# Attention and two gated layers on one core: first loads in another order, early weight conversions placed one head later

## The chip, the cores and the metric

The kernel runs on one core of a Trainium2 chip. The metric is the device time of one execution in microseconds (us); the median of three runs of the kernel before is 1163.88 us.

## The reference, cut to what matters

Four batches of 8 heads, 576 tokens, head width 64: causal attention with a bias from running sums of `s`, then two gated layers of width 512 and inner width 1536 over all 2304 tokens.

```python
scores = scale * np.matmul(q, k.transpose(0, 1, 3, 2))
cum = np.cumsum(np.maximum(s, 0.0), axis=-1)
bias = -(cum[:, :, :, None] - cum[:, :, None, :])
scores = np.where(causal, -1e9, scores + np.minimum(bias, 0.0))
attn = softmax(scores)
x = np.matmul(attn, v)            # -> [2304, 512]
x = (sigmoid(x @ w_gate) * (x @ w_val)) @ w_out
return ((x @ w_a) * (x @ w_b)) @ w_out2
```

The weights arrive as 8-byte floats; the kernel converts them to pairs of 4-byte parts (high and low).

## The kernel before, in words

The kernel has two stages one after the other: `attention()`, 32 heads, and `mlps()`, the two layers. Both write their work as named operations of a `Schedule` (line 27): an engine, a function, the operations that it depends on, and a priority, which is a planned time. For attention the operations are given out with `in_order=True` (lines 47 to 69): of all operations whose dependences have been given out, the one with the smallest priority goes next. So the priority alone sets the order in which each engine (TensorE, VectorE, ScalarE, GpSimd) and each queue of DMA issues works, and every one of them works strictly in that order. An instruction that waits holds back all that stands behind it on its engine. SyncE (SP) issues nearly all loads; ScalarE issues two small transfers per head.

Priorities are counted in planned heads of `HT` = 6.1; head i starts at `t0 = HT * i`. For each head there are, in the order of the data:

- `lqk` (load_qk, line 337) brings q and k of a head into one of three tiles `r`; `lv` (lines 341, 342) brings v in two DMAs into one of two tiles `vx`;
- `hq1`, `hk1` (lines 472, 473) round them on ScalarE into `o`; `hk2`, `hq2` (474, 475) copy them by DMA into the second tile; `lok`, `loq` (476, 478) write the rounding rests on VectorE. The load of q and k for head i waits for these four of head i-3;
- `rel` (482, 483) brings the bias rows of a head by two DMAs. For the first three heads `relk` and `relq` (416, 439) write them directly from the running sums (`sums`, lines 406 to 411, then `relh` 434 and `rell` 435);
- `S` (498, 503): TensorE makes scores in two groups, `mx` (511): VectorE takes their maxima, `mT` (518) turns them, `mc` (520) copies them on ScalarE, `md` (522) sends them by DMA into `o`;
- `ST` (535, 536): scores again, transposed; `ex` (541): exp on ScalarE; `cs` (557): causal mask on GpSimd; `pv` (570): times v; `xc` (579) copies out, `sd`, `rd`, `rb` (581, 603, 600) bring the row sums round by DMA, and `xm` (583) divides on GpSimd.

The score groups share one PSUM tile, so group 1 of a head can start only when the maxima of group 0 are taken, and the next head's group 0 only after those of group 1.

Among the heads, eleven weight tiles are prepared (`weights`, line 253; the loop at 609): one load (line 205 or 210, 512 KB, SP queue) every three heads, with priority `HT * (3 * e - 2)` for tile e, and then steps: `mag` (224, ScalarE), two steps into `u` (225, 227, VectorE), two more on VectorE (229, 232), the copy (243, ScalarE) and the rest (244, GpSimd). Their places are the entries of the list `at`, counted from the load's place: the first three steps stood one head after the load, the next two two and three heads after it.

At the very start, SP issues `s` (line 403, read once per group of rows, so four times over), then q and k of three heads, then the constants of the first two heads (`selectors`, lines 380, 381, two DMAs each), whose data GpSimd makes.

Of the kernel before, what the change touches and what calls it, by code (L numbers as in the profile page):

```python
# [22 lines left out]
def f32(ap):  # L23
    return ap.bitcast(FP32)


class Schedule:
# [9 lines left out]
    def op(self, name, eng, dur, fn, deps, prio, acq=None, rel=None, lat=None):  # L37
        rel = () if rel is None else rel if isinstance(rel[0], tuple) else (rel,)
        self.ops[name] = (eng, dur, fn, deps, prio, acq, rel, self.LAT if lat is None else lat)
# [80 lines left out]
def attn_mlp_kernel(  # L120
# [14 lines left out]
    nc = tc.nc  # L135
# [39 lines left out]
    early = [(i, m) for m in range(2) for i in range(3)] + [(3, 0), (3, 1)]  # L175
# [77 lines left out]
    def weights(sc, n, m, deps, prio, part=None, at=None):  # L253


        key = (n, m)
        steps = w_steps(n, m)
        nv = len(steps) - 2
        prev = ("wl",) + key
        sc.op(prev, "SP", 0.0 if part == 1 else 0.5, lambda: None if part == 1 else w_load(n, m), deps, prio,  # L260
              acq=("raw", key), lat=0.0 if part == 1 else WLAT)
        for k, (eng, d, fn) in enumerate(steps):
            if part is not None and (k < nv) != (part == 0):
                continue
            last = k == len(steps) - 1
            name = ("wr" if last else "w%d" % k,) + key
            sc.op(name, eng, d, fn, [prev], prio + (at[k + 1] if at else 0.01 * k), acq=("u", key) if nv and k == 0 else None,
                  rel=(("u", key),) if nv and k == nv - 1 else ("raw", key) if last else None)
            prev = name
# [20 lines left out]
    def attention():  # L290
        with ExitStack() as c2:
            def tile1(shape, dtype, name):
                return alone(c2, shape, dtype, name, side="right")
# [12 lines left out]
            NO, NR2, NX = 4, 3, 5  # L306
# [19 lines left out]
            o_t = [tile1([128, CK1 + S], F32R, f"o{i}") for i in range(NO)]  # L326
# [7 lines left out]
            sel, neg1 = ya_sb[0:NR, 1, 2 * S:3 * S], ya_sb[0:3, 1, 3 * S:4 * S]  # L334

            def load_qk(i):
                nc.sync.dma_start(out=r_t[i % NR2], in_=qk[i])

            def load_v(i):
                v, e = vx_t[i % 2], i % 2  # L340
                nc.sync.dma_start(out=v[:, 0:4, e * D:(e + 1) * D], in_=vm[i // 4, :, i % 4])
                nc.sync.dma_start(out=v[0:TL, 4, e * D:(e + 1) * D], in_=vt[i // 4, :, i % 4])
# [36 lines left out]
            def selectors(o):  # L379
                nc.sync.dma_start(out=f32(o[D:R1, CQ1:CQ1 + S]), in_=sel[:, None].to_broadcast([NR, 2, S]))  # L380
                nc.sync.dma_start(out=f32(o[R1:KB + 1, CK1:CK1 + S]), in_=neg1)
# [10 lines left out]
            op = sc.op  # L392
# [34 lines left out]
            op("ms1", "Pool", 1.2, lambda: nc.gpsimd.memset(f32(o_t[1][D:2 * D]), 0.0), ["masks"], -270)  # L427
            op("mkb", "ACT", 0.7, masks_b, ["masks"], -280)
            for j in range(NR2):
                op(("lqk", j), "SP", 0.6, lambda j=j: load_qk(j), ["s"], -290 + j, lat=3.0)  # L430
            for j in range(2):
                op(("sel", j), "SP", 1.3, lambda j=j: selectors(o_t[j]), [("lqk", j), "selc", "ms1"], -260 + j, lat=2.2)
            op("sums", "DVE", 2.7, sums, ["s"], -250)
            op("relh", "ACT", 0.67, lambda: nc.scalar.copy(out=rel[:, 0], in_=cum), ["sums"], -230)
            op("rell", "DVE", 0.7, lambda: nc.vector.tensor_tensor(
                out=rel[:, 1], in0=cum, in1=f32(rel[:, 0]), op=ALU.subtract), ["relh"], -220)
            op("more", "DVE", 5.0, more, ["rell"], -219)
            for i, (name, eng) in enumerate((("Pool", nc.gpsimd), ("ACT", nc.scalar), ("SP", nc.sync))):
                op(("relk", i), "SP", 0.65, lambda i=i: nc.sync.dma_start(
                    out=f32(o_t[i][D:R1, CK1:CK1 + S]), in_=f32(rel[i:NR * BH:BH])), ["rell", "more"], -210 + i, lat=2.2)  # L440
                for c in range(NR):
                    op(("relq", i, c), name, 0.6, lambda i=i, c=c, eng=eng: relq(eng, i, c), ["rell", "more"], -200 + i, lat=2.2)
            for c in range(NR):
                op(("rels", c), "Pool", 0.6, lambda c=c: relq_store(c), ["rell"], -20, lat=2.2)
            op("relk", "SP", 1.2, lambda: nc.sync.dma_start(
                out=relk_d.rearrange("b c e s -> c b e s"), in_=f32(rel)), ["rell"], -190, lat=2.5)
# [5 lines left out]
            HT = 6.1  # L452
# [5 lines left out]
            def head(i):  # L458
                b, h = divmod(i, H)
                t0 = HT * i  # L460
                o, o2, r, vx, pt = o_t[i % NO], p_t[i % 3], r_t[i % NR2], vx_t[i % 2], pt_t[i % 3]
                nm, mr = nm_t[i % 4], mr_t[i % 3]
                k1, q1, k2, q2 = o[:, CK1:CK1 + S], o[:, CQ1:CQ1 + S], o2[:, S:2 * S], o2[:, 0:S]
                up, dn = slice(0, D), slice(D, 2 * D)
                done = [("ST", i - NO, c) for c in range(NC)] + [("S", i - NO, g) for g in range(2)]
                done2 = [("ST", i - 3, c) for c in range(NC)]

                if i >= NR2:
                    op(("lqk", i), "SP", 0.7, lambda: load_qk(i),
                       [(w, i - NR2) for w in ("hq1", "hk1", "lok", "loq")], t0 - 4 * HT + 4.6, lat=3.0)  # L470
                op(("lv", i), "SP", 0.9, lambda: load_v(i), [("pv", i - 2, 1), ("sel", 1)], t0 + 4.0, lat=3.0)
                op(("hq1", i), "ACT", 0.65, lambda: nc.scalar.copy(out=q1[up], in_=r[up]), [("lqk", i)] + done, (-255, -229, -228)[i] if i < NR2 else t0 - 3 * HT + 5.2)
                op(("hk1", i), "ACT", 0.65, lambda: nc.scalar.copy(out=k1[up], in_=r[dn]), [("lqk", i)] + done, (-255, -229, -228)[i] if i < NR2 else t0 - 3 * HT + 5.2)
                op(("hk2", i), "ACT", 0.7, lambda: nc.scalar.dma_start(out=f32(k2[dn]), in_=f32(k1[up])), [("hk1", i)] + done2, t0 - 2 * HT + 0.05)
                op(("hq2", i), "SP", 0.5, lambda: nc.sync.dma_start(out=f32(q2[up]), in_=f32(q1[up])), [("hq1", i)] + done2, t0 - 2 * HT + 0.1)
                op(("lok", i), "DVE", 0.9, lambda: nc.vector.tensor_tensor(
                    out=k2[up], in0=r[dn], in1=f32(k2[dn]), op=ALU.subtract), [("hk2", i)], t0 - HT + 3.0)
                op(("loq", i), "DVE", 0.9, lambda: nc.vector.tensor_tensor(
                    out=q2[dn], in0=r[up], in1=f32(q1[up]), op=ALU.subtract), [("hq1", i)] + done2, t0 - HT - 0.5)
# [11 lines left out]
                for g, cs in ((0, (3, 2, 0)), (1, (1, 4))):  # L491
# [31 lines left out]
                    out=f32(o[KB:KB + 1, CQ1:CQ1 + 640]), in_=f32(mr)), [("mc", i)] + done, t0 - HT + 3.6, lat=2.2)  # L523
# [39 lines left out]
                def pv(reg):  # L563
# [14 lines left out]
                x, j = xt[i % NX], i // 2  # L578
# [5 lines left out]
                    out=x_sb[own, h // 2, b * S:(b + 1) * S], in0=x[own], in1=rb_t[j % 2][own], op=ALU.mult),  # L584
# [21 lines left out]
            for i in range(NH):  # L606
                head(i)

            for e, key in enumerate(order[:len(early) + NRAW]):
                split = [3 * HT + 1.6, 3 * HT + 4.6] if e < len(early) else [0, 0]  # L610
                weights(sc, *key, [("S", 3 * e - 3, 0)], HT * (3 * e - 2), part=None if e < len(early) else 0,
                        at=[0, HT + 1.2, HT + 1.9, HT + 2.5, 2 * HT + 1.9, 3 * HT + 1.9] + split)

            for k in range(KD):
                t0 = HT * (NH - 12 + k)
                op(("x0h", k), "ACT", 0.4, lambda k=k: nc.scalar.copy(out=xs0[:, 0, k], in_=x_sb[:, k, 0:NB]), [("xm", i) for i in range(H)], t0 + 1.7)
                op(("x0l", k), "DVE", 0.5, lambda k=k: nc.vector.tensor_tensor(
                    out=xs0[:, 1, k], in0=x_sb[:, k, 0:NB], in1=f32(xs0[:, 0, k]), op=ALU.subtract), [("x0h", k)], t0 + 2.6)
# [157 lines left out]
    with tc.manual_schedule():  # L776
        attention()
        mlps()
# [45 lines left out]
```

## Time and profile before

| | |
|---|---|
| runs of the kernel before | 1162.53, 1163.88, 1164.17 us |
| profiled execution | 1162.06 us, its span 1160.3 us |
| attention | about 0 to 245 us of the span |
| the two layers | to 1160 us |
| TensorE busy, whole span | 1104.7 us (95%) |
| VectorE, ScalarE, GpSimd busy | 633.2, 357.3, 294.7 us |

Times in the rows are microseconds from the start of the span. A line of the timeline gives start, duration, engine, line of the kernel, operation, what is written and read, and in brackets how long the engine stood idle before and what ended that. SPq and ACTq are the issue queues of SyncE and ScalarE; a DMA's duration there is that of its issue, not of its data.

### The profile page before, as it was taken

The numbers are of one execution on the slowest core, as the hardware profiler recorded it, in microseconds if no ns is written. First come the engines' busy times: TensorE is split into PE (matmuls) and PEld (weight loads), VectorE is DVE, ScalarE is ACT, GpSimd is POOL, SyncE is SP. The second block draws the span as 40 slices with busy tenths as digits, with TensorE's granted clock in tenths as the row PEclk, the third lists the DMA queues.
The fourth block names the chain that finished last, engine by engine and source line by source line (L and its number), as shares of the span: only waits on it lengthen the run. The fifth ranks groups of instructions, "written<-read, shape, count | busy, mean of one in ns | idle before, by whom it ended". The sixth has DMA issues, their size and how long they took to land.

```text
span 1160.3 us, 16120 instructions
## 1 busy us (share of the span) xinstructions
PE 1104.7 (95%) x6152; PEld 1038.0 (89%) x6152; DVE 633.2 (55%) x1015; ACT 357.3 (31%) x635; POOL 294.7 (25%) x364
## 2 busy tenths in 40 slices
PE   1699989999999999999999999999999999999998
PEld 1587777788999999999999999899999999999997
DVE  4787887728323694337963358622487334653322
ACT  2475665634222441113321124322243111221100
POOL 2245445454100341002420023310133111211100
PEclk9999999999999999999999999999999999999999
DMA  3566665614100231001320012200033000200001
GB/s 102 130 165 170 166 162 148 167 52 127 38 1 1 74 109 37 1 1 55 100 64 1 1 38 91 91 1 1 20 95 105 1 1 1 73 28 28 28 28 55
DMA packets 69743, 74.08 MB, mean 64 GB/s; under 512 B 28551, under 2 KB 53311, under 8 KB 69666
## 3 DMA queue, kind: packets, MB, share of 16 engines
q1 hardware_dynamic: 66514, 68.08, 20.1%
q10 hardware_dynamic: 2896, 4.81, 1.8%
q8 instruction: 49, 0.80, 0.3%
q14 instruction: 28, 0.23, 0.1%
q0 software_dynamic: 256, 0.15, 0.1%
HBM read 57.65 MB, written 5.60 MB: 55 GB/s over the span
## 4 chain that ended last, share of the span: by engine, by line
PE 76%; DVE 8%; DMA 6%; issue 4%; POOL 3%; ACT 1%; SPq 1%; ACTq 0%; POOLq 0%; DVEq 0%
PE ps L277 23%; PE ps L278 23%; PE ps L276 23%; PE ps_x L570 4%; PE ps_g L498 1%; DVE u L227 1%; DVE u L225 1%; DMA raw<-in_moe_w_out_dram 1%; POOL w L244 1%; DVE h L716 1%; DVE raw L232 1%; DVE hf L702 1%; DVE raw L229 1%; POOL x_sb L583 1%; PE ps_e L535 1%
## 5 line engine op out<-in xcount | busy, mean ns | idle before, releaser
L276 PE MATMUL ps<-xs,w 128*128 128x384 f32 x1152 | 385.0, 334 | 0.0
L278 PE MATMUL ps<-xs,w 128*128 128x384 f32 x1152 | 385.0, 334 | 0.0
L277 PE MATMUL ps<-xs,w 128*128 128x384 f32 x1152 | 384.9, 334 | 0.0
L713 POOL TENSOR_SCALAR h<-hf 128x384 fp32r<-128x384 f32 x144 | 92.1, 640 | 576.5 <-DVE hf L702 576.5
L702 DVE TENSOR_TENSOR hf<-ps,g 128x384 f32<-128x384 f32 x144 | 80.0, 555 | 280.9 <-PE ps L278 278.5
L276 PEld LDWEIGHTS ps<-xs,w 128*128 128x128 f32 x1152 | 216.3, 188 | 0.7
L277 PEld LDWEIGHTS ps<-xs,w 128*128 128x128 f32 x1152 | 216.2, 188 | 0.7
L278 PEld LDWEIGHTS ps<-xs,w 128*128 128x128 f32 x1152 | 216.2, 188 | 0.0
L698 ACT ACTIVATE g<-ps 128x384 f32<-128x384 f32 x144 | 70.7, 491 | 434.2 <-PE ps L278 434.1
L716 DVE TENSOR_TENSOR h<-hf,h 128x384 fp32r<-128x384 f32 x144 | 88.9, 618 | 83.0 <-POOL h L713 83.0
L244 POOL TENSOR_TENSOR w<-raw,w 128x512 fp32r<-128x512 f32 x72 | 99.8, 1387 | 133.1 <-ACT w L243 128.6
L276 PE MATMUL ps<-h,w 128*128 128x384 f32 x288 | 97.3, 338 | 2.4 <-POOL h L713 1.8
L278 PE MATMUL ps<-h,w 128*128 128x384 f32 x288 | 97.0, 337 | 1.8 <-POOL w L244 1.8
L570 PE MATMUL ps_x<-pt,vx 128*128 128x320 f32 (+4 forms) x448 | 97.2, 369 | 1.1 <-ACT xt L579 1.0
L277 PE MATMUL ps<-h,w 128*128 128x384 f32 x288 | 97.1, 337 | 0.6 <-DVE h L716 0.6
L570 PEld LDWEIGHTS ps_x<-pt,vx 128*128 128x128 f32 x448 | 77.2, 194 | 18.8 <-ACT xt L579 1.3
L511 DVE TENSOR_REDUCE nm<-ps_g 128x1 f32<-128x512 f32 (+4 forms) x160 | 77.0, 531 | 29.4 <-PE ps_g L503 29.4
L277 PE MATMUL ps<-w,h 128*128 128x512 f32 x216 | 84.6, 392 | 1.0 <-POOL w L244 0.9
L276 PE MATMUL ps<-w,h 128*128 128x512 f32 x216 | 84.1, 389 | 0.3 <-ACT w L243 0.3
L278 PE MATMUL ps<-w,h 128*128 128x512 f32 x216 | 84.4, 391 | 0.0
L498 PE MATMUL ps_g<-o 128*128 128x512 f32 (+2 forms) x192 | 45.2, 346 | 40.3 <-DVE nm L511 18.4
L557 POOL TENSOR_SCALAR_AFFINE_SELECT pt<-pt 128x256 f32<-128x256 f32 (+1 forms) x96 | 48.7, 526 | 129.1 <-ACT pt L541 127.8
(92 smaller groups left out, 1323.1 us busy)
## 6 DMA issues: line engine op xcount, KB each, us to landing
raw<-in_moe_w_out_dram SPq DMA_DIRECT2D x24, 512.0 KB
r<-in_qk_dram SPq DMA_DIRECT2D x32, 288.0 KB
raw<-in_moe_w_gate_dram SPq DMA_DIRECT2D x12, 512.0 KB
raw<-in_moe_w_val_dram SPq DMA_DIRECT2D x12, 512.0 KB
raw<-in_moe_w_a_dram SPq DMA_DIRECT2D x12, 512.0 KB
raw<-in_moe_w_b_dram SPq DMA_DIRECT2D x12, 512.0 KB
o<-o ACTq DMA_DIRECT2D x32, 144.0 KB
o<-o SPq DMA_DIRECT2D x32, 144.0 KB
```

The costliest lines, as they stand in the source:

```text
L244: ("Pool", 1.23, lambda: nc.gpsimd.tensor_tensor(out=wtile(n, m)[:, 1], in0=value(), in1=f32(wtile(n, m)[:, 0]), op=ALU.subtract)),
L276: nc.tensor.matmul(out=outp, lhsT=wh, rhs=xh, start=(e == 0), stop=False)
L277: nc.tensor.matmul(out=outp, lhsT=wh, rhs=xl, start=False, stop=False)
L278: nc.tensor.matmul(out=outp, lhsT=wl, rhs=xh, start=False, stop=(e == n - 1))
L498: nc.tensor.matmul(out=ps[0:n, p0 + k0:p0 + k0 + kn], lhsT=q1[:, 128 * c:nk], rhs=k1[:, k0:k0 + kn], start=c in first or (c == 4 and k0 == ...
L511: nc.vector.tensor_reduce(out=nm[0:n, c:c + 1], in_=ps[0:n, p0:p0 + nk], axis=AX.X, op=ALU.max)
L557: nc.gpsimd.affine_select(to, to, [[0, 2], [1, n]][2 - w:], ALU.is_ge, 0.0, base=0, channel_multiplier=-1)
L570: nc.tensor.matmul(out=px[:, 256 + a:256 + q1_], lhsT=vx[:, j], rhs=pt[:, p0:p0 + q1_ - a], start=j == 0, stop=j == js[-1])
L698: op(("g", i, c), "ACT", 0.06 + N * 0.00083, lambda c=c, g=g: nc.scalar.activation(out=sc.get("g", (i, c))[:, 0:N], in_=sc.get("ps", g)[:, ...
L702: op(("hf", i, c), "DVE", 0.07 + N * 0.00104, lambda c=c, u=u: nc.vector.tensor_tensor(out=sc.get("hf", (i, c))[:, 0:N], in0=sc.get("ps", ...
L713: op(("hh", i, c), "Pool", 0.245 + N * 0.00083, lambda c=c, src=src: nc.gpsimd.tensor_scalar(sc.get("h", (i, c))[:, 0, 0:N], src(), 1.0, 1 ...
L716: op(("hl", i, c), "DVE", 0.07 + N * 0.00104, lambda c=c, src=src: nc.vector.tensor_tensor(out=sc.get("h", (i, c))[:, 1, 0:N], in0=src(), ...
```

## The change

Three things move; nothing is added or removed. At the start, the constants of the first head are issued ahead of q and k of head 0, those of the second head ahead of q and k of heads 1 and 2, and the constants no longer name the load of q and k among their dependences. The load of v is placed at 4.8 instead of 4.0 within its head, which is behind the head's issue of `sd` (4.5) and of `lqk` (4.6) instead of ahead of them. And all seven conversion steps of the weights stand one `HT` later, while their loads stay where they are.

```diff
             for j in range(NR2):
-                op(("lqk", j), "SP", 0.6, lambda j=j: load_qk(j), ["s"], -290 + j, lat=3.0)
+                op(("lqk", j), "SP", 0.6, lambda j=j: load_qk(j), ["s"], -259.5 + j, lat=3.0)
             for j in range(2):
-                op(("sel", j), "SP", 1.3, lambda j=j: selectors(o_t[j]), [("lqk", j), "selc", "ms1"], -260 + j, lat=2.2)
+                op(("sel", j), "SP", 1.3, lambda j=j: selectors(o_t[j]), ["selc", "ms1"] if j else ["selc"], -260 + j, lat=2.2)
...
-                op(("lv", i), "SP", 0.9, lambda: load_v(i), [("pv", i - 2, 1), ("sel", 1)], t0 + 4.0, lat=3.0)
-                op(("hq1", i), "ACT", 0.65, ..., (-255, -229, -228)[i] if i < NR2 else t0 - 3 * HT + 5.2)
-                op(("hk1", i), "ACT", 0.65, ..., (-255, -229, -228)[i] if i < NR2 else t0 - 3 * HT + 5.2)
+                op(("lv", i), "SP", 0.9, lambda: load_v(i), [("pv", i - 2, 1), ("sel", 1)], t0 + 4.8, lat=3.0)
+                op(("hq1", i), "ACT", 0.65, ..., (-251, -229, -228)[i] if i < NR2 else t0 - 3 * HT + 5.2)
+                op(("hk1", i), "ACT", 0.65, ..., (-251, -229, -228)[i] if i < NR2 else t0 - 3 * HT + 5.2)
...
-                split = [3 * HT + 1.6, 3 * HT + 4.6] if e < len(early) else [0, 0]
+                split = [4 * HT + 1.6, 4 * HT + 4.6] if e < len(early) else [0, 0]
                 weights(sc, *key, [("S", 3 * e - 3, 0)], HT * (3 * e - 2), part=None if e < len(early) else 0,
-                        at=[0, HT + 1.2, HT + 1.9, HT + 2.5, 2 * HT + 1.9, 3 * HT + 1.9] + split)
+                        at=[0, 2 * HT + 1.2, 2 * HT + 1.9, 2 * HT + 2.5, 3 * HT + 1.9, 4 * HT + 1.9] + split)
```

## Rows read from the trace of the kernel before

**Rows 1.** Busy time by stretch: start:end, length, engines' busy us, granted clock, DMA share, GB/s

```profile
60.00:100.00 40.00, 40.00 (x247) 33.41 (x246) 32.93 (x61) 27.70 (x52) 18.98 (x27) 1.00 0.65 168
100.00:235.00 135.00, 123.60 (x735) 101.58 (x733) 108.66 (x191) 81.27 (x152) 65.88 (x86) 0.99 0.62 161
...
171.00:176.00 5.00, 5.00 (x20) 3.59 (x19) 3.83 (x8) 2.08 (x5) 3.89 (x4) 0.66 0.65 159
275.00:1160.00 885.00, 877.58 (x4838) 848.91 (x4837) 441.82 (x670) 210.82 (x367) 172.58 (x200) 1.00 0.12 40
```

**Rows 2.** Timeline, the first 20 us

```profile
0.80 0.76 SPq L403 DMA_DIRECT2D ya_sb<-in_s_dram  x1
...
1.61 1.37 SPq L337 DMA_DIRECT2D r<-in_qk_dram  x3
...
3.61 0.75 SPq L380 DMA_DIRECT2D o<-ya_sb  x1
...
8.48 0.46 DVE L406 TENSOR_SCALAR ya_sb<-ya_sb 128x576 f32<-128x576 f32 x1 [4.97 <-DMA ya_sb<-in_s_dram]
...
9.08 0.67 ACT L472 CAST o<-r 64x576 fp32r<-64x576 f32 x1 [4.71 <-DMA r<-in_qk_dram]
...
11.42 0.67 ACT L434 CAST ya_sb<-ya_sb 128x576 fp32r<-128x576 f32 x1 [0.99 <-DVE ya_sb L411]
...
16.95 1.19 PE L498 MATMUL ps_g<-o 128*128 128x512 f32 x3 [16.95 <-DMA o<-ya_sb]
```

**Rows 3.** DMA, first 12 us in 40 slices of 0.3 us: GB/s

```profile
GB/s 0 0 0 0 0 0 0 31 8 77 200 261 353 207 207 146 246 346 215 200 207 207 161 92 54 69 84 100 100 100 100 100 100 100 31 0 0 0 0 0
```

**Rows 4.** Timeline, 22 to 43 us: the first weight tile and heads 0 to 2

```profile
22.67 0.37 PE L518 MATMUL ps_t<-idf,nm 128*5 128x128 f32 x1 [1.26 <-DVE nm L511]
...
25.33 0.95 SPq L205 DMA_DIRECT2D raw<-in_moe_w_gate_dram  x1
26.32 2.78 SPq L475 DMA_DIRECT2D o<-o  x2
32.07 0.68 ACT L224 ACTIVATE mag<-raw 128x512 f32<-128x512 f32 x1 [17.32 <-DMA raw<-in_moe_w_gate_dram]
32.08 0.43 DVE L225 TENSOR_SCALAR u<-raw 128x512 int32<-128x512 int32 x1 [9.55 <-DMA raw<-in_moe_w_gate_dram]
32.54 0.69 DVE L227 SCALAR_TENSOR_TENSOR u<-raw,u 128x512 int32<-128x512 int32 x1
...
33.26 0.75 DVE L476 TENSOR_TENSOR o<-r,o 64x576 fp32r<-64x576 f32 x1
...
33.94 1.34 DVE L511 TENSOR_REDUCE nm<-ps_g 128x1 f32<-128x512 f32 x3
...
35.33 1.06 PE L498 MATMUL ps_g<-o 128*128 128x256 f32 x3 [10.78 <-DVE nm L511]
...
39.49 0.78 PE L535 MATMUL ps_e<-o 128*128 128x512 f32 x1
...
42.44 0.63 PE L498 MATMUL ps_g<-o 128*128 128x256 f32 x3
```

**Rows 5.** TensorE's waits, 60 to 250 us: us in total, times, longest

```profile
PE ps_g L498 <- DVE nm L511: 6.2, 5, 2.3
PE ps_g L498 <- DMA o<-relq_d: 3.4, 3, 2.0
```

**Rows 6.** VectorE's waits, 60 to 250 us: for weight tiles

```profile
DVE u L225 <- DMA raw<-in_moe_w_gate_dram: 3.2, 2, 1.7
DVE u L225 <- DMA raw<-in_moe_w_out_dram: 3.0, 2, 2.0
```

**Rows 7.** The SP queue's waits, 60 to 235 us

```profile
SPq L342 <- DMA o<-mr: 14.3, 6, 4.1
SPq L581 <- DMA raw<-in_moe_w_gate_dram: 5.7, 3, 2.9
```

**Rows 8.** Timeline, 95 to 108 us: the issue of a load of v

```profile
104.16 0.48 SPq L342 DMA_DIRECT2D vx<-in_vt_dram  x1
```

More of the change, by code (lines that the diff above doesn't have):

```diff
@@ L470, in head @@
                        [(w, i - NR2) for w in ("hq1", "hk1", "lok", "loq")], t0 - 4 * HT + 4.6, lat=3.0)
-                op(("lv", i), "SP", 0.9, lambda: load_v(i), [("pv", i - 2, 1), ("sel", 1)], t0 + 4.0, lat=3.0)
-                op(("hq1", i), "ACT", 0.65, lambda: nc.scalar.copy(out=q1[up], in_=r[up]), [("lqk", i)] + done, (-255, -229, -228)[i] if i < NR2 else t0 - 3 * HT + 5.2)
-                op(("hk1", i), "ACT", 0.65, lambda: nc.scalar.copy(out=k1[up], in_=r[dn]), [("lqk", i)] + done, (-255, -229, -228)[i] if i < NR2 else t0 - 3 * HT + 5.2)
+                op(("lv", i), "SP", 0.9, lambda: load_v(i), [("pv", i - 2, 1), ("sel", 1)], t0 + 4.8, lat=3.0)
+                op(("hq1", i), "ACT", 0.65, lambda: nc.scalar.copy(out=q1[up], in_=r[up]), [("lqk", i)] + done, (-251, -229, -228)[i] if i < NR2 else t0 - 3 * HT + 5.2)
+                op(("hk1", i), "ACT", 0.65, lambda: nc.scalar.copy(out=k1[up], in_=r[dn]), [("lqk", i)] + done, (-251, -229, -228)[i] if i < NR2 else t0 - 3 * HT + 5.2)
                 op(("hk2", i), "ACT", 0.7, lambda: nc.scalar.dma_start(out=f32(k2[dn]), in_=f32(k1[up])), [("hk1", i)] + done2, t0 - 2 * HT + 0.05)
```

## The prediction

> **What bounds the kernel now.** I read the busy times by stretch first. From 275 us on, the two layers keep TensorE busy 877.58 of 885.00 us, and nothing of the change lies there, so whatever attention saves or loses reaches the end whole [rows 1]. Within attention TensorE is busy 40.00 of 40.00 us from 60 to 100, and 123.60 of 135.00 from 100 to 235 [rows 1]. So there are two places to gain: the first 40 us, in which TensorE has hardly begun, and some 11 us of holes after 100.
>
> Next the timeline of the start. TensorE's first scores begin at 16.95, when the bias rows have landed; these come from the sums over s, which wait for s until 8.48, and ScalarE starts on q and k of head 0 at 9.08 [rows 2]. The DMA rate shows why s is late: between 200 and 353 GB/s in the burst of s and three loads of q and k, then a flat 100 GB/s from 8.1 to 10.2 [rows 3]. Then TensorE stands idle for 10.78 us before 35.33. Its releaser is a maximum on VectorE, but that is only the end of a queue: VectorE stood 9.55 us and ScalarE 17.32 us in front of the first weight tile, which SP issued at 25.33 and which landed at 32.07 [rows 4]. Behind it stood the copy `mc` of head 0, `lok` of head 0 (33.26) and the maxima of head 1 (33.94), none of which needs a weight [rows 4].
>
> Last the waits after 60 us. TensorE waits 6.2 us in five places for maxima and 3.4 us in three for bias rows [rows 5]; VectorE waits 3.2 and 3.0 us in four places for weight tiles [rows 6]; SP waits long for landings of transfers that its next DMA doesn't read, 14.3 us for `md` before the second half of v, 5.7 us for a weight tile before `sd` [rows 7]. I read that as a limited number of landings that can be outstanding: a slow weight load holds up whatever is issued some places behind it.
>
> **The change part by part: first loads.** Now s goes alone. It is 128 rows of 2304 bytes, 295 KB. At the flat 100 GB/s it takes 2.9 us; first bytes move at 2.1 to 2.4 us [rows 3], so it lands near 5.6 instead of 8.46. At the burst's 353 GB/s it would be 3.4, and without any gain 8.46; I take 5.6, since the flat rate is that of few transfers left over. The sums took 8.48 to 11.42 [rows 2], so they end at 8.6. But the next step, `relh` on ScalarE, stands behind `hq1` and `hk1` of head 0. Their load is issued behind two DMAs of constants, 3.61 plus twice about 0.8, at 5.2 [rows 2]; with the same 1.4 us to its first bytes and 200 GB/s it lands at 8.1, at 100 GB/s at 9.5. Two steps of 0.67 [rows 2] make `relh` start at 9.5 (bound: 10.9) instead of 11.42. I take 1.7 us earlier, between 0.5 and 1.9, for the first scores, and for everything that SP issues behind the bias rows: the weight load at 23.6, landed by the same 6.74 us [rows 4] at 30.3. The constants' wait for GpSimd costs nothing: SP waited until 3.61 for it before too [rows 2].
>
> **The first weight tile.** Its step `mag` gets priority 1.2, which puts it behind `mc` of head 0 (-2.55) and ahead of `mc` of head 1 (3.55); the first step into `u` gets 1.9, behind the second maxima of head 1 (0.7) and ahead of `lok` of head 1 (3.0). So `mc` of head 0 follows its transpose at 22.67 + 0.37 - 1.7 = 21.3, `lok` of head 0 and the maxima of head 1 follow without the weights, and VectorE reaches `u` near 27. There it still waits, some 3.3 us instead of 9.55. From 30.3: 0.43 + 0.69 for the two steps, 0.75 for `lok` and 1.34 for the maxima of head 2 [rows 4] end at 33.5, and the second scores of head 2 start at 33.6 instead of 42.44 [rows 4]. TensorE comes out the same way: the transposed scores of head 0 need `hq2`, issued right behind the weight load on SP, so about 30.5, and the group took 42.44 - 39.49 = 2.95 us [rows 4]: 33.5. ScalarE's exp waits for q and k of head 3, issued near 27.5 and landing about 2 us behind the weights, plus 1.34 us of rounding: 33.7. Three engines agree within half a microsecond: 42.44 - 33.6 = 8.8; I take **8.6**, 1.7 from the first loads and 6.9 from here. If s brings only 0.5 it is 7.4; if all of 1.9, 8.8. From there TensorE is full [rows 1], so the shift stays.
>
> **The other conversions.** The ten later tiles' steps are as many and as long; each set meets one head later, when the load has landed. That takes away VectorE's 6.2 us of waits [rows 6] and ScalarE's beside them. What it is worth to TensorE lies between 0 and the 6.2 us that it waited for maxima [rows 5]; I take **3.0**, half, because the waits for bias rows come from another queue and will end later than some of the removed ones: 3.4 us of them are there already [rows 5]. The single `u` and `mag` stay free in time (released at 4 HT + 1.9, next taken at 5 HT + 1.2), as do the three `raw` tiles. The last tile's step on VectorE lies at 32 HT, ahead of the last reciprocal at 34 HT: hidden; uncovered it would be 0.7 us.
>
> **The load of v** goes behind `sd` and q and k on SP. Where SP waits for `sd` (ScalarE's copy out), the two issues of v, 0.48 each [rows 8], no longer fill that wait and `hq2` and the bias rows go out up to 1.0 us later. Where SP is held by a weight tile's landing, it's v that is held, which has about a head to spare, and no longer q and k. I take 0 for both together, with ends of +1.0 per weight load at worst and -1 in all at best.
>
> Sum: 8.6 + 3.0 = 11.6 us. The profiled execution took 1162.06 us (span 1160.3), 1.8 below the median; 1162.06 - 11.6 = 1150.5, and against the median of 1163.88 it is **1152.3**.
>
> **The rivals.** (a) *SP paces the middle.* The conversions' waits go, but the bias rows, behind the weight load on SP, end TensorE's waits a moment later. For it: SP's long waits for landings [rows 7], and that TensorE's holes begin only after 100 us though weights are loaded before, as if slack were used up [rows 1]. Against: TensorE's larger waits are for maxima [rows 5]. Gain 8.6 alone: 1155.3.
>
> (b) *s lands no earlier alone.* The load of s may be held by the few DMA engines that serve it, whatever runs beside it. The flat 100 GB/s at the end of the burst [rows 3] would then be its own pace all along. `relh` then starts at 8.48 + 2.94 = 11.42 as before, the 1.7 go, and 6.9 + 3.0 give 1154.0. Against: 295 KB at 100 GB/s end at 5.4, not 8.46, so something beside it slowed it. The Trainium skill, page DMA: Bandwidth & Descriptors, section Rules for kernel authors, says that a leading broadcast dimension of c copies confines a DMA to at most c engines; s has four such copies. By that rule q and k on the other engines would leave s alone, and the sum would be 9.9 instead of 11.6.
>
> (c) *All holes go.* TensorE's waits for maxima and bias rows, 6.2 + 3.4 [rows 5], vanish, and with them the stretch at a granted clock of 0.66 from 171 to 176, (1 - 0.66) x 5 = 1.7 us [rows 1]: 8.6 + 9.6 + 1.7 = 19.9, 1144.0. Against: the bias rows' queue isn't relieved.
>
> (d) *The first wait only moves.* VectorE and ScalarE still stand before the first tile until 30.3. If what stands behind them then (`lok` of head 1, `mc` of head 1, q and k of head 4) is the true start of the pipeline, only the 1.7 and the two steps' 1.1 plus one set of maxima of 1.3 are won: 4.1, 1159.8. Against: the work behind the wait was head 0's and head 1's [rows 4], which now goes ahead of it.
>
> (e) *Given back.* From 60 us on the DMAs move 168 and 161 GB/s [rows 1]; if that were the limit over all of attention, the start would be won and lost again later: within 2 us of 1163.9. Against: a share of 0.65 busy, 0.62 later.
>
> (f) *Slower.* v behind q and k puts the bias rows 1.0 us later in each head with a weight load. It decides where those rows already end TensorE's wait [rows 5], and where a wait grows long enough to bring the clock to half, as at 171: 8 loads x (1.0 + 1.7) = 21.6, less 8.6: 1176.9. It needs four such heads to eat the start. Against: one such stretch in all of attention before [rows 1].
>
> **How the numbers follow.** A measurement here can tell about 0.2%, 2.3 us. Chances: the forecast 0.39, (a) 0.25, (b) 0.12, (c) 0.10, (d) 0.06, (e) 0.05, (f) 0.03. The first five, 0.92, are faster; (e) is no change; (f) slower. The forecast's own range is 1149 to 1155; a range of 1145 to 1160 takes in (a), (b), (d) and what of (c) stops short of all holes, and leaves out (e) and (f).
>
> **What would show it.** Right: TensorE's idle of 10.78 us gone, the second scores of head 2 near 33.6, VectorE's first wait for a weight tile 2 to 4 us and none after it; the first sums near 5.6; q and k at ScalarE near 8.1. Wrong: sums still at 8.5 (b), TensorE's waits for bias rows grown from 3.4 to 6 us or more (a), more stretches of half clock (f). The forecast fails if the second scores of head 2 come after 36, or if the holes from 100 to 235, then 8 us earlier, stay at 11 us.

## The result and the profile after

The changed kernel takes 1150.15 us (median of 4 runs, 1149.07 to 1154.16) against 1163.2 us for the kernel before (median of 4 runs). The ratio on record is 0.9895, 95% interval 0.9869 to 0.9922; the two medians by themselves give 0.9888. The profiled execution took 1150.44 us, its span 1148.7: 11.6 us less than the profiled execution before, and 11.6 us was the sum of the forecast. The sum came out, but not every term of it; the parts of this section say which.

**The start.** The timeline of the kernel after, its first 42 us (columns as in [rows 2]; an SPq line is the issue of a DMA):

```profile
6.50 0.46 DVE L406 TENSOR_SCALAR ya_sb<-ya_sb 128x576 f32<-128x576 f32 x1 [2.99 <-DMA ya_sb<-in_s_dram]
...
8.19 0.67 ACT L472 CAST o<-r 64x576 fp32r<-64x576 f32 x1 [3.82 <-DMA r<-in_qk_dram]
...
8.87 0.67 ACT L473 CAST o<-r 64x576 fp32r<-64x576 f32 x1
8.89 0.52 DVE L411 TENSOR_SCALAR ya_sb<-ya_sb,small 128x576 f32<-128x576 f32 x1
9.57 0.67 ACT L434 CAST ya_sb<-ya_sb 128x576 fp32r<-128x576 f32 x1
...
15.12 1.19 PE L498 MATMUL ps_g<-o 128*128 128x512 f32 x3 [15.12 <-DMA o<-ya_sb]
...
20.72 0.75 DVE L476 TENSOR_TENSOR o<-r,o 64x576 fp32r<-64x576 f32 x1
...
23.36 0.87 SPq L205 DMA_DIRECT2D raw<-in_moe_w_gate_dram  x1
...
29.09 0.43 DVE L225 TENSOR_SCALAR u<-raw 128x512 int32<-128x512 int32 x1 [2.35 <-DMA raw<-in_moe_w_gate_dram]
...
30.23 0.76 PE L536 MATMUL ps_e<-o 128*128 128x512 f32 x1 [0.64 <-DMA o<-o]
...
33.04 1.04 PE L498 MATMUL ps_g<-o 128*128 128x256 f32 x3
...
35.88 1.19 PE L498 MATMUL ps_g<-o 128*128 128x512 f32 x3
...
37.07 0.78 PE L535 MATMUL ps_e<-o 128*128 128x512 f32 x1
```

The sums over s begin at 6.50 instead of 8.48 [rows 2]. `relh` (L434) begins at 9.57 instead of 11.42 and now stands right behind `hk1`, which ends at 9.54; the sums end just ahead of that, at 9.41. The first scores begin at 15.12 instead of 16.95. The weight load is issued at 23.36 instead of 25.33 [rows 4]. The work that stood behind the first weight tile goes ahead of it: `lok` of head 0 at 20.72 instead of 33.26 [rows 4]. VectorE's wait at `u` shrinks from 9.55 to 2.35 us, and TensorE's hole of 10.78 us is gone: 0.64 us is left, in front of `hq2`'s copy at 30.23.

**A part of that is not kept.** The second scores of head 2 begin at 33.04 instead of 42.44, 9.4 us earlier. The first product with v, some 8 us of work later, is only 6.6 us earlier. TensorE's rows at the end of that work, first after, then before:

```profile
40.32 1.04 PE L498 MATMUL ps_g<-o 128*128 128x256 f32 x3
...
41.55 2.98 PE L570 MATMUL ps_x<-pt,vx 128*128 128x256 f32 x14
```

```profile
44.76 0.70 PE L498 MATMUL ps_g<-o 128*128 128x512 f32 x3
...
45.40 0.48 PE L535 MATMUL ps_e<-o 128*128 128x512 f32 x1
...
48.14 2.98 PE L570 MATMUL ps_x<-pt,vx 128*128 128x256 f32 x14
```

The scores of head 3 took 0.70 us before (at 44.76) and 1.19 after (at 35.88); the first transposed scores behind them 0.48 and 0.78. So this work ran at the lower of TensorE's two levels, 1.2 GHz, where it ran at 2.4 GHz before. The durations fall to the fast ones at about the same time in both kernels: the 128x256 scores take 1.06 us at 35.33 and 0.63 at 42.44 before [rows 4], and 1.04 us still at 40.32 after. The trace's first entry of the granted clock, at full speed in both, stands at 42.08 us before and at 41.44 after. (The busy times read 1.00 from 30 to 42 us all the same, because the time ahead of the first entry is counted as 1.00.) The change brought the work forward, but not the clock.

From the second scores of head 2 to the first product with v it is 8.51 us after (33.04 to 41.55) and 5.70 before (42.44 to 48.14). The busy times of that stretch (columns as in [rows 1]) after, before, and in x3, the kernel before with only v moved:

```profile
33.04:41.55 8.51, 7.25 (x31) 5.68 (x30) 4.83 (x9) 5.66 (x10) 2.51 (x4) 1.00 0.65 182
42.44:48.14 5.70, 4.40 (x31) 3.43 (x30) 4.61 (x8) 3.15 (x7) 3.16 (x4) 1.00 0.76 205
43.07:51.60 8.53, 7.26 (x31) 5.70 (x30) 4.54 (x8) 4.49 (x9) 2.69 (x5) 1.00 0.51 151
```

The same 31 matmuls take 7.25 us after and 4.40 before: that is the 2.8 us given back. x3 begins as the kernel before does and takes 8.53 us all the same; its first entry of the clock stands at 55.0. In the table below the same stretch takes 5.70 to 5.85 us in before, x1 and x8, and 7.50 to 8.83 in all other kernels without extra matmuls. So what the clock takes back differs between executions too, and the 2.8 us hold for this pair of profiles.

**The middle.** The busy times by stretch of the kernel after (columns as in [rows 1]) and TensorE's waits from 45 to 242 us:

```profile
60.00:100.00 40.00, 38.94 (x237) 32.25 (x235) 32.53 (x60) 26.94 (x51) 21.05 (x28) 1.00 0.68 173
100.00:235.00 135.00, 127.13 (x757) 104.78 (x758) 105.33 (x187) 83.39 (x155) 71.72 (x90) 1.00 0.64 155
```

```profile
PE ps_g L498 <- DVE nm L511: 2.8, 4, 1.2
PE ps_g L498 <- DMA o<-relq_d: 2.6, 2, 1.4
PE ps_g L498 <- DMA o<-relk_d: 1.3, 2, 1.1
PE ps_x L570 <- DMA vx<-in_vm_dram: 1.1, 3, 0.5
PE ps_x L570 <- ACT xt L579: 1.0, 1, 1.0
```

Two waits of the kernel before, 60 to 250 us, that [rows 5] and [rows 6] leave out:

```profile
PE ps_g L498 <- DMA o<-relk_d: 1.4, 1, 1.4
DVE u L225 <- DMA raw<-in_moe_w_val_dram: 1.4, 1, 1.4
```

TensorE is busy 127.13 us from 100 to 235 instead of 123.60. Its waits for maxima fell from 6.2 to 2.8 us; those for bias rows fell little, from 4.8 us (3.4 for `relq` [rows 5] and 1.4 for `relk`) to 3.9; a wait for v, 1.1 us, is new. VectorE waits for no weight tile after the first, where it waited 7.6 us in all (6.2 [rows 6] and 1.4). ScalarE waits 3.0 us for q and k instead of 8.1. From the first product with v to that of the last head it is 193.06 us (41.55 to 234.61) instead of 197.58 (48.14 to 245.72): 4.5 us won. All of TensorE's waits together shrank by 3.5 us, from 12.3 (60 to 250 us) to 8.8 (45 to 242 us), and the stretch of lower clock from 171 to 176 [rows 1] isn't there in this execution, 1.7 us; the two make 5.2, 0.7 more than was won. With the 6.6 us up to the first product and 0.5 behind the last one (914.58 to 914.09) the 11.6 us are complete.

**The DMA rate**, GB/s in slices of 0.3 us from 0 to 12 us, with s and the constants of the first head up to 6.3 and q and k after that:

```profile
GB/s 0 0 0 0 0 0 0 31 84 92 108 108 100 84 46 92 100 108 61 54 54 246 215 292 223 31 8 115 146 230 392 330 415 277 62 0 0 0 0 0
```

Without q and k beside it, s moves at 84 to 108 GB/s, with falls to 46 and 54. The Trainium skill, page DMA: Bandwidth & Descriptors, section Rules for kernel authors, says that a leading broadcast dimension of c copies confines a DMA to at most c engines; the trace agrees with that for the four copies of s: the mean busy share of the 16 DMA engines is 0.23 from 2.1 to 6.3 us, and 0.72 from 6.3 to 10.2, where q and k reach up to 415 GB/s. The flat stretch of [rows 3] has the same rate, but it is not s: it lasts from 8.1 to 10.2 us, and s had landed by 8.46. Which transfers moved in it, no run shows.

### The profile page after: what moved, and what is told of

Same layout as the page of the kernel before. It is cut to its first block, busy times and chain, and to the rows that moved or that the text cites. A ratio compares the mean times of both kernels' runs of the same rounds, so it can differ in the third digit from the quotient of the medians.

```text
span 1148.7 us, 16112 instructions
## 1 busy us (share of the span) xinstructions
PE 1107.2 (96%) x6152; PEld 1039.6 (91%) x6152; DVE 631.2 (55%) x1015; ACT 357.7 (31%) x635; POOL 299.9 (26%) x364
## 4 chain that ended last, share of the span: by engine, by line
PE 78%; DVE 8%; DMA 5%; POOL 3%; issue 3%; ACT 2%; SPq 0%; ACTq 0%; POOLq 0%; DVEq 0%
PE ps L277 22%; PE ps L278 22%; PE ps L276 22%; PE ps_x L570 5%; PE ps_g L498 2%; DVE u L227 2%; POOL w L244 1%; DVE raw L229 1%; DVE h L716 1%; DVE hf L702 1%; DVE raw L232 1%; PE ps_e L535 1%; PE ps_e L536 1%; DVE u L225 1%; PE ps_g L503 1%
## 5 line engine op out<-in xcount | busy, mean ns | idle before, releaser
L557 POOL TENSOR_SCALAR_AFFINE_SELECT pt<-pt 128x256 f32<-128x256 f32 (+1 forms) x96 | 51.5, 558 | 114.4 <-ACT pt L541 113.7
L243 ACT CAST w<-raw 128x512 fp32r<-128x512 f32 x72 | 47.2, 659 | 104.6 <-DVE raw L232 103.0
```

The costliest lines, as they stand in the source:

```text
L243: ("ACT", 0.53, lambda: nc.scalar.copy(out=wtile(n, m)[:, 0], in_=value())),
L557: nc.gpsimd.affine_select(to, to, [[0, 2], [1, n]][2 - w:], ALU.is_ge, 0.0, base=0, channel_multiplier=-1)
```

## The experiments

Each kernel was timed beside the kernel before, and the ratio is to its runs of the same series. All times are us; the last five columns are from the profiled execution of each: start of `u` (the first weight tile has landed), second scores of head 2, first product with v, that of the last head, span.

| kernel | ratio to before | 95% interval | `u` | scores h2 | v first | v last | span |
|---|---|---|---|---|---|---|---|
| before | 1 | | 32.08 | 42.44 | 48.14 | 245.72 | 1160.3 |
| after | 0.9895 | 0.9869–0.9922 | 29.09 | 33.04 | 41.55 | 234.61 | 1148.7 |
| x1 first loads only | 0.9965 | 0.9951–0.9979 | 30.34 | 40.89 | 46.74 | 246.27 | 1161.9 |
| x2 conversions only | 0.9925 | 0.9904–0.9945 | 33.53 | 37.18 | 44.7 | 236.28 | 1150.6 |
| x3 v only | 0.9996 | 0.9981–1.0011 | 32.4 | 43.07 | 51.60 | 249.88 | 1163.4 |
| x4 all but v | 0.9899 | 0.9881–0.9918 | 29.25 | 33.2 | 41.05 | 238.42 | 1152.9 |
| x5 first tile only | 0.9958 | 0.9944–0.9972 | 33.45 | 36.95 | 45.48 | 244.69 | 1159.3 |
| x6 all but the ten other tiles | 0.9933 | 0.9918–0.9949 | 30.02 | 33.99 | 41.49 | 240.93 | 1156.3 |
| x7 after, TensorE kept busy | 0.9893 | 0.9875–0.991 | 32.42 | 35.94 | 42.13 | 234.08 | 1148.6 |
| x8 before, TensorE kept busy | 0.9994 | 0.9981–1.0007 | 32.02 | 40.97 | 46.67 | 245.44 | 1160.9 |
| x9 weight loads behind bias rows | 0.9854 | 0.9834–0.9874 | 28.91 | 32.87 | 40.98 | 232.66 | 1147.3 |
| x10 = x11 and TensorE kept busy | 0.9918 | 0.9901–0.9934 | 33.25 | 36.51 | 43.1 | 235.82 | 1151.1 |
| x11 store behind the small copies | 0.9926 | 0.9911–0.9941 | 35.26 | 38.52 | 46.63 | 238.11 | 1152.6 |
| x12 = x9, v back at 4.0 | 0.9856 | 0.9831–0.9882 | 28.96 | 32.91 | 41.74 | 233.48 | 1148.7 |

### The three parts by themselves: x1 to x4

x1 is the kernel before with the first loads alone:

```diff
-    op(("lqk", j), ..., ["s"], -290 + j, lat=3.0)
+    op(("lqk", j), ..., ["s"], -259.5 + j, lat=3.0)
-    op(("sel", j), ..., [("lqk", j), "selc", "ms1"], -260 + j, lat=2.2)
+    op(("sel", j), ..., ["selc", "ms1"] if j else ["selc"], -260 + j, lat=2.2)
```

(`hq1`, `hk1` go from -255 to -251 with it.)

> The kernel before with the new order of the first loads alone. Theory (the sum's terms hold apart): first scores near 15.1 instead of 16.95, the first weight tile lands 1.8 earlier, near 30.2, and everything behind it moves by just that; second scores of head 2 near 40.6; time 1.8 us less, 0.998 of before. Rival (the start only pays together with the conversions, because what it wins is lost in front of the weight tile): scores at 15.1 but second scores of head 2 still near 42.4, time as before.

x2 is the kernel before with the conversions alone:

```diff
-    split = [3 * HT + 1.6, 3 * HT + 4.6] ...
-    at=[0, HT + 1.2, HT + 1.9, HT + 2.5, 2 * HT + 1.9, 3 * HT + 1.9] + split
+    split = [4 * HT + 1.6, 4 * HT + 4.6] ...
+    at=[0, 2 * HT + 1.2, 2 * HT + 1.9, 2 * HT + 2.5, 3 * HT + 1.9, 4 * HT + 1.9] + split
```

> The kernel before with all conversions one head later, nothing else. Theory: the idle of 10.78 us before the second scores of head 1 goes; second scores of head 2 near 34.9 (42.4 less 7.5), no wait of VectorE for weight tiles after the first; time 9 to 11 us less, 0.991. Rival (v's place carries the middle of attention): the start's 7 us come, but the holes from 100 to 235 stay at 11 us, time 6 to 7 less, 0.994.

x3 is the kernel before with v alone, and x4 the kernel after with v put back:

```diff
-    op(("lv", i), ..., t0 + 4.0, lat=3.0)
+    op(("lv", i), ..., t0 + 4.8, lat=3.0)
```

> The kernel before with the load of v behind q and k alone. Theory (v's place is worth nothing by itself): within 1 us of before, SP's waits for sd's data up, ScalarE's waits for q and k down. Rival (bias rows come 1 us later in heads with a weight load): 3 to 8 us slower, TensorE's waits for bias rows from 5 to 9 us or more. Second rival (q and k ahead of the held-up place is what relieves the middle): 2 to 4 us faster.

> The changed kernel with the load of v put back in front. Theory (v's place is worth nothing): within 1 us of the changed kernel, 0.989 of before; TensorE's waits for v (1.1 us in the changed kernel) go, its waits for maxima or bias rows grow by about as much. Rival (v's place carries 2 us or more): 0.991 or worse.

The first loads are worth 0.35%, 4.1 us (2.4 to 5.7), the conversions 0.75%, 8.7 us, v nothing (0.9996, and x4 stands at 0.9899 beside 0.9895). 4.1 + 8.7 is 12.8 us, and the whole change measured 1.05%, 12.2: the parts add up. x1's rival, that nothing is won without the conversions, falls. The first loads brought more than the forecast's 1.7 and more than they show in the profile of x1, where the first scores come 1.4 us earlier (15.53) and `u` 1.7. By x4 against x2 they are worth 3.0 us (0.9899 and 0.9925), uncertain by about as much, which doesn't rule out 1.7. The rest is not accounted for; that execution was the slowest of twelve (1163.68, the others down to 1155.91), with a mean granted clock of 0.97 from 100 to 235 against 0.99 [rows 1].

x2's time lies between its theory (0.991) and its rival (0.994), but the rival's mechanism fails: TensorE is busy 128.35 us from 100 to 235, so the holes shrank from 11.4 to 6.7 us without v's new place. Its second scores of head 2 came at 37.18, where 34.9 was expected; there the weight tile landed at 33.53, 1.5 us later than before.

That v is worth nothing is no absence of effect. TensorE's waits from 45 to 242 us in x4, beside those of the kernel after:

```profile
PE ps_g L498 <- DMA o<-relq_d: 5.4, 4, 1.7
PE ps_g L498 <- DMA o<-relk_d: 1.8, 1, 1.8
PE ps_g L498 <- DVE nm L511: 1.5, 1, 1.5
```

With v ahead of `sd`, the bias rows cost 7.2 us and the maxima 1.5, 8.7 in all; with v behind q and k they cost 3.9 and 2.8, plus 1.1 for v, 7.8 in all. ScalarE's waits for q and k are 9.6 us in x4 and 3.0 after. One order makes the bias rows late, the other v.

### The first tile against the ten others: x5, x6

x5 puts only the first tile's conversions a head later, on the kernel before; x6 is the kernel after with the ten others put back:

```diff
+    L = HT if e == 0 else 0
+    split = [L + 3 * HT + 1.6, L + 3 * HT + 4.6] ...
+    at=[0, L + HT + 1.2, L + HT + 1.9, L + HT + 2.5, L + 2 * HT + 1.9, L + 3 * HT + 1.9] + split
```

> The kernel before with the steps of the first weight tile alone one head later. Theory (the first tile carries the start, the other ten the holes of the middle): second scores of head 2 near 35 to 37 as in the run with all conversions later, but the waits for maxima in the middle stay at 6 us; time 5 to 6.5 us less, 0.995 of before. Rival (the middle is paced by SP and its landings, so the ten others bring nothing): as with all conversions later, 0.9925.

> The changed kernel with the steps of tiles 1 to 10 put back where they were. Theory: it loses the 3 us that the other conversions bring, 0.992 of before, with TensorE's waits for maxima between 45 and 245 us back at 6 us or more from 2.8. Rival (SP paces the middle): 0.9895, waits for bias rows in place of those for maxima.

TensorE's waits from 45 to 242 us in x5, then in x6:

```profile
PE ps_g L498 <- DVE nm L511: 6.6, 7, 1.7
...
```

```profile
PE ps_g L498 <- DVE nm L511: 4.5, 5, 1.8
PE ps_g L498 <- DMA o<-relq_d: 4.3, 3, 2.5
PE ps_g L498 <- DMA o<-relk_d: 2.4, 2, 1.6
```

The first tile alone gives 0.42%, 4.9 us. Its second scores of head 2 come 5.5 us earlier (36.95), its first product with v 2.7 (45.48): here too the slow clock takes back half. The waits for maxima stay, 6.6 us as against 6.2 [rows 5]. In x6 they come back to 4.5 us and not to the 6 or more that were expected; the bias rows take 6.7 there instead of 3.9. The ten others are worth 3.8 us by x2 against x5 (0.9925, 0.9958) and 4.4 by the kernel after against x6 (0.9895, 0.9933), though in each of these pairs the intervals touch. So the two subtractions agree on some 4 us, uncertain by about 3, where rival (a) had 0 and the forecast 3.0. The start by itself is worth 7.8 us (5.9 to 9.5) by x6, and 9.0 by x1 and x5 added.

### The clock of the start: x7, x8, x10, x11

x7 and x8 give TensorE work whose product nothing reads, 95 small matmuls before the first scores and in the gaps of the first heads, on the kernel after and before:

```diff
+    def warm(n):
+        px = sc.pools["px"][0]
+        for _ in range(n):
+            nc.tensor.matmul(out=px[:, 0:256], lhsT=idb, rhs=mkb, start=True, stop=True, ...)
+    for k, (n, at) in enumerate([(60, -9.0), (7, -8.6), (7, -6.0), (7, -2.5), (7, 0.1), (7, 6.2)]):
+        op(("wm", k), "PE", 0.1 * n, lambda n=n: warm(n), ["mkb"], at)
```

> The changed kernel with 95 small matmuls that nothing reads in TensorE's holes of the first 36 us: 60 ahead of the first scores, 7 in each of five waits for maxima. Theory (the changed kernel wins 9.4 us up to the second scores of head 2, but only 6.6 at the first product with v, because TensorE's granted clock still rises to full only at 41.4 us, as before at 42.1): scores and products of heads 0 and 1 run at the full clock, the first product with v starts near 38 instead of 41.55, time 2.5 to 3.5 us less than the changed kernel, 0.9865 of before. Rival (the start is held by VectorE and the landings, not by TensorE's clock): the first product with v within 1 us of 41.5, time as the changed kernel.

> The kernel before with the same 95 matmuls. Theory: of the start before, TensorE waits for the weight tile until 35.3 and cools down meanwhile, so little is won: 0 to 2 us, 0.999 of before. Rival (the clock is worth as much before as after): 3 us less, 0.997.

Neither changed the time. x7 stands at 0.9893 beside 0.9895: its theory (0.9865) failed and its rival holds, in the time and in the first product with v (42.13). x8 stands at 0.9994, as its theory had it; the rival's 0.997 lies outside the interval. In x7 the clock did rise sooner, but the weight tile landed later and the clock fell again. Its timeline, SP's waits from 15 to 34 us, and the busy times from 30 to 36 us:

```profile
27.25 0.70 SPq L381 DMA_DIRECT2D o<-ya_sb  x1
...
28.00 0.42 SPq L205 DMA_DIRECT2D raw<-in_moe_w_gate_dram  x1
...
28.50 0.48 PE L535 MATMUL ps_e<-o 128*128 128x512 f32 x1
...
32.42 0.43 DVE L225 TENSOR_SCALAR u<-raw 128x512 int32<-128x512 int32 x1 [6.82 <-DMA raw<-in_moe_w_gate_dram]
...
33.12 0.77 PE L536 MATMUL ps_e<-o 128*128 128x512 f32 x1 [4.14 <-DMA o<-o]
```

```profile
SPq L381 <- DMA relk_d<-ya_sb: 4.2, 1, 4.2
```

```profile
30.00:36.00 6.00, 2.88 (x12) 2.73 (x12) 3.49 (x7) 2.02 (x4) 0.00 (x0) 0.50 0.80 207
```

The transposed scores of head 0 take 0.48 us (28.50), 2.4 GHz, instead of 0.78. But SP's issue of a constant waits 4.2 us for the landing of the store `relk_d`, 576 KB, which that constant doesn't read; the weight load behind it goes out at 28.00 instead of 23.36. TensorE then waits 4.14 us for `hq2`, the granted clock is 0.50 from 30 to 36 us, and the work at 33.12 runs slow again (0.77 us). From the second scores of head 2 to the first product with v x7 takes 6.19 us (35.94 to 42.13), where the kernel after takes 8.51 and the kernel before 5.70. So the matmuls kept the clock up for a part of the start only. The stretch shows what the clock costs there; that the whole time would fall by it is not shown.

x11 therefore issues the constants and the first two `hq2` ahead of that store, and x10 does this with the matmuls:

```diff
-    op(("sel", j), ..., ["more"], -180 + j, lat=2.2)
+    op(("sel", j), ..., ["more"], -196 + j, lat=2.2)
-    op(("hq2", i), ..., [("hq1", i)] + done2, t0 - 2 * HT + 0.1)
+    op(("hq2", i), ..., [("hq1", i)] + done2, -192 + i if i < 2 else t0 - 2 * HT + 0.1)
```

> The same order on SP without the small matmuls. Theory of the clock: TensorE no longer waits 0.64 us for the second copy of q of head 0, but the clock still rises only near 40; first product with v between 40.5 and 41.5, time 0 to 1 us less than the changed kernel. Rival (landings set the start): first product with v at 38 to 39.5, 2 to 3.5 us less.

> The changed kernel with the 95 small matmuls, and on SP the constants of heads 2 and 3 and the second copies of q of heads 0 and 1 issued ahead of the 576 KB store of bias rows, so that the store's landing holds none of them. Theory of the clock: the transposed scores of heads 0 and 1 run at full clock, the first product with v starts at 38 to 39.5 instead of 41.55, time 2 to 3.5 us less than the changed kernel, 0.987. Rival (landings and VectorE set the start): first product with v between 40.5 and 42, as in the run without the matmuls.

Both expectations failed: 0.9926 for x11 and 0.9918 for x10, no faster than the kernel after (the intervals overlap with its own), and first products with v at 46.63 and 43.1. The timeline of x11:

```profile
20.34 0.61 SPq L445 DMA_DIRECT2D relk_d<-ya_sb  x1
...
21.54 1.51 SPq L205 DMA_DIRECT2D raw<-in_moe_w_gate_dram  x1
...
35.26 0.43 DVE L225 TENSOR_SCALAR u<-raw 128x512 int32<-128x512 int32 x1 [8.19 <-DMA raw<-in_moe_w_gate_dram]
...
36.12 0.31 PE L535 MATMUL ps_t<-o 128*64 128x64 f32 x1 [1.88 <-ACT mr L520]
```

The weight load is issued 1.8 us sooner than after, and its first reader starts 6.2 us later: 13.7 us from issue to use (21.54 to 35.26) instead of 5.7 (23.36 to 29.09). The store now stands 1.2 us ahead of it on the queue, instead of 7.5 us. TensorE had `hq2` in time, and then waited for ScalarE, whose steps stand behind `mag`. What the new order of the small transfers won, the later landing of the weight tile lost; whether it was the store alone that delayed the tile is not separated from the other transfers that moved. From the second scores of head 2 to the first product with v x10 takes 6.59 us (36.51 to 43.1) and x11 8.11 (38.52 to 46.63): 1.5 us between them, although x10 too ran that stretch only in part at full speed (granted clock 0.70).

### The bias rows' queue: x9, x12

x9 is the kernel after with the ten later weight loads 2.1 later, behind the bias rows of their head; the conversions stay where they are:

```diff
+    Q = 2.1 if e else 0
-    weights(..., HT * (3 * e - 2), ..., at=[0, 2 * HT + 1.2, ...] + split)
+    weights(..., HT * (3 * e - 2) + Q, ..., at=[x - Q for x in [0, 2 * HT + 1.2, ...] + split])
```

> The changed kernel with the loads of weight tiles 1 to 10 placed 2.1 later in their head, right behind the bias rows of the head instead of ahead of them; the conversions stay. Theory (bias rows end TensorE's waits in the middle because they queue behind the 512 KB weight load): TensorE's waits for bias rows between 45 and 245 us fall from 3.9 to under 1.5 us, VectorE still never waits for a weight tile, 1 to 4 us less than the changed kernel, 0.987 of before. Rival (the SP queue's slots pace the middle whatever the order): waits for bias rows stay at 3 to 5 us, time within 1 us of the changed kernel.

TensorE's waits from 45 to 242 us in x9:

```profile
PE ps_x L570 <- DMA vx<-in_vm_dram: 3.1, 3, 2.0
PE ps_g L498 <- DVE nm L511: 2.5, 3, 1.3
PE ps_x L570 <- ACT xt L579: 1.0, 1, 1.0
```

The waits for bias rows, 3.9 us in the kernel after, are gone; those for v grew by 2.0 us, from 1.1 to 3.1. The ratio is 0.9854 (0.9834 to 0.9874), 0.4% below that of the kernel after, though the two intervals overlap by a little. So it was the weight load ahead of them on SP that made the bias rows late; that its new place also saves time is probable, but the overlap leaves it open.

x12 is x9 with v back at 4.0:

> The run with the weight loads behind the bias rows, and the load of v put back to 4.0, ahead of sd and of q and k. Theory (behind the weight load, v is what TensorE waits for now: 3.1 us in three places in that run's profile, none before the change): waits for v go, those for bias rows stay away, 1 to 2.5 us less than that run, 0.984 of before. Rival (v is only exchanged for q and k at the place that a weight load holds up): ScalarE's waits for q and k and TensorE's for maxima grow by as much, time within 1 us of that run, 0.985.

TensorE's waits in x12, same stretch:

```profile
PE ps_g L498 <- DVE nm L511: 3.0, 2, 1.6
PE ps_t L518 <- ACT pt L541: 2.3, 2, 1.3
PE ps_x L570 <- ACT xt L579: 1.0, 1, 1.0
PE ps_x L570 <- DMA vx<-in_vm_dram: 0.6, 1, 0.6
```

The waits for v fall from 3.1 to 0.6 us, but 2.3 us for ScalarE's exp come in, since ScalarE stands longer in front of its rounding of q and k (6.3 us, 3.3 of them put down to their own load, against 3.8 in x9). The ratio is 0.9856: an exchange, as in x3 and x4. Both x9 and x12 are below the kernel before and, by their medians, below the kernel after.

## Why the prediction was right, and where not

The median came out at 1150.15 us against 1152.3 forecast. Step by step:

- **First loads, 1.7 us.** Right in the first scores (1.8 us earlier) and in the weight load (2.0 earlier), by another split. q and k landed at 8.19, where 8.1 was forecast, and `relh` began at 9.57, where 9.5 was; but s landed at 6.50 and not near 5.6 (the forecast's own figures, 2.4 + 2.9, give 5.3). The forecast took 100 GB/s from the flat stretch of [rows 3], which is not s; the rate was about right, and the falls below it made the difference. They cost nothing: with `hk1` ending at 9.54, a landing of s at 5.6 would have moved `relh` by at most 0.1 us. Rival (b) falls with the 2.0 us by which s landed earlier without q and k; what holds of it is the low rate that s has even then. For the total, x1 measured 4.1 us; what goes beyond the 1.7 is open.
- **First weight tile, 6.9 us.** The chain was right: `u` waits 2.35 us (3.3 forecast, 2 to 4 given as the test), the load took 5.7 us instead of 6.74, `hq2` of head 0 ended TensorE's last wait at 30.23 (30.5 forecast), and the second scores of head 2 came at 33.04 (33.6). The step that failed is its last sentence, "From there TensorE is full, so the shift stays." Full is not fast: the work brought forward ran at 1.2 GHz, and 9.4 us became 6.6. Where the forecast had 8.6 for the start, the start brought 6.6 in the profiled pair. The timed runs don't show this shortfall: they give the start 7.8 us (x6) or 9.0 (x1 and x5), with 8.6 inside the uncertainty. So the loss is shown for one pair of executions, and its mean over many is open.
- **Other conversions, 3.0 us.** Right within what can be measured: 3.8 and 4.4 us by the two subtractions, uncertain by about 3, and 4.5 in the profile with 1.7 of the clock in it, which leaves 2.8. The mechanism stood: VectorE waits for no later tile (7.6 us before, where the prediction read 6.2), TensorE's waits for maxima fell by 3.4 us, which is close to the half of 6.2 that was taken, and 3.9 us for bias rows were left.
- **Load of v, 0.** Right in the sum (x3, x4), and not by absence: it moved waits from ScalarE and the bias rows to `sd` and v.
- **Rivals.** (a), that SP's queue keeps the middle from gaining, falls: waits for bias rows didn't grow and the ten tiles brought about 4 us. Half of it was true, as x9 shows: the weight load on that queue was behind the 3.9 us of waits for bias rows that were left. (c) had that gain too, but not by this change. (d) and (e) fall with the 33.04 and the 4.5. (f) needed longer waits for bias rows and more stretches of lower clock; the profile after has none from 100 to 235 (1.00 against 0.99).

So that the profiled pair came out at just 11.6 us is luck: the start brought 2.0 us less than forecast, and 1.7 us came from a stretch of lower clock that the profile before had and the profile after had not, which the forecast counted for its rival (c) only and which comes and goes between executions. That the gain is near 12 us is not luck: the chain of the start and the waits of the middle changed as forecast, and the parts timed by themselves add up to it.

## What to carry to other kernels

When a wait at the start is removed, ask at which clock the work behind it will run: time won in front of work that runs at the lower clock is not all kept, and in the profiled pair 2.8 of 9.4 us went that way. On an engine that works in order, a step whose transfer lands late holds back work that needs nothing of it; put the step where its data has landed, and the small, urgent transfers of the same queue ahead of the large one (x9). When moving one load only exchanges one wait for another (x4, x12), look at what large transfer stands beside it: in x9 moving that one took the waits for bias rows away.

## What was not expected of the hardware

- A load can take much longer close behind another large transfer on its queue: 512 KB took 13.7 us to its first reader behind a 576 KB store issued 1.2 us earlier (x11), and 5.7 us in the kernel after, 7.5 us behind the store.
- An issue can wait for a landing whose data it doesn't use: 4.2 us in x7. The prediction read this as a limit on outstanding landings; whether the chip or the program sets one, no run shows.
- The time at which the clock rises differs between executions whose starts are alike. In x3, of which only the place of v differs from the kernel before, the first product with v still ran slow at 51.6 us (4.66 us instead of 2.98 for the same 14 matmuls), and the clock's first entry stands at 55.0 us instead of 42.08:

```profile
47.10 0.78 PE L535 MATMUL ps_e<-o 128*128 128x512 f32 x1
...
51.60 4.66 PE L570 MATMUL ps_x<-pt,vx 128*128 128x256 f32 x14
56.13 0.71 PE L498 MATMUL ps_g<-o 128*128 128x512 f32 x3
```

- The mean granted clock from 100 to 235 us lay between 0.96 (x8) and 1.00 (after, x2, x7, x11), with 0.97 in x1, x4 and x6: 0.04 of 135 us is 5 us, as much as one part of this change. A single profile can't price such a part; many runs can, here to 2 or 3 us.
